# Attention values with the values as weights: outputs as columns, sums by ones, inverses by 32x32 turns

## The chip, the core and the metric

The kernel runs on one core of one Trainium2 chip. The metric is the device time of one execution in microseconds. A core has five engines that run side by side and wait for each other through semaphores: TensorE (matmuls, PE in the profile, its weight loads PEld), VectorE (DVE), ScalarE (ACT), GpSimd (POOL) and SyncE (SP, which here only issues DMAs). TensorE writes to PSUM[...].

## What is computed

For 8 batches and 12 heads of 64, over 448 tokens: q and k are normalised by their root mean square, attention is taken, the heads of a token are put side by side (768), and a feed-forward layer follows with w_in (768 x 2048) and w_out (2048 x 768).

```
q_n, k_n = rmsnorm(q, g_q), rmsnorm(k, g_k)
attn = exp(scale * q_n @ k_n.T);  attn = attn / sum(attn)
x = concat_heads(attn @ v)                  # 3584 x 768
h = x @ w_in
out = (h * sigmoid(1.702 * h)) @ w_out      # 3584 x 768
```

## The kernel before

**Units.** Two heads of one batch make a pair; 48 pairs in all, six for each batch. The six pairs of batch 0 are cut into two half units each (224 queries), the other 42 pairs are one unit (448 queries). Keys come in four chunks of 112 tokens.

**One unit.** The tasks have letters, and the letters stand in the lists that follow. L loads rows (lines 876 to 883). S, R and Q square, reduce and invert the norms; N (line 942) scales the rows; T turns them on TensorE (line 963), KQ and K copy the turned rows out. V casts the values (line 949). C is the score (line 995): keys as weights, 64 rows for each head, queries streamed, so scores come with keys on partitions. E is the exponential on ScalarE (line 1011), written as `att`.

P is the product with the values (line 1021). There the exponentials are the weights (a window of 128 queries) and the values are streamed, 65 columns wide: 64 of a head and one column of ones, which gives the sum. Four chunks of keys accumulate into one window, so there are 32 matmuls in a whole unit and 16 in a half unit, 1536 in all. The output `o` has queries on partitions. A unit's P is cut into `w` (two in a whole unit, one in a half) and x (four of four matmuls each), 96 (unit, w) and 384 tasks. O (line 1034) takes the reciprocal of the sums and multiplies, on VectorE, into `obs`. B (line 1051) turns `obs` on TensorE so that channels lie on partitions, into one of the work banks "w". X (line 1058) copies it to `xT`, on VectorE or ScalarE. The bank for `o` is a single one: the next P with x = 0 waits for the last O.

**The rest.** F is the product with w_in (line 1218), H a tanh on ScalarE, G the gate on VectorE (line 1237); the product with w_out is made partly in the plain way (Y, line 1251) and otherwise in seven products in place of eight (P1 to P7, lines 1315 to 1322, with sums S1 to S5 and copies X1 to X5 and U); the last two batches share the same scheme for w_in (J, line 1601). D stores rows.

**Order.** Every engine's order is written out in the table ORDER from line 218 on: one list of task names for each engine. `od.add(...)` gives each task its engine, a length that the planner assumes, and what it depends on; `run` then emits the tasks in the order of the lists. So TensorE's order is fixed: value products stand between products of the feed-forward layer. For the score the planner assumes `190 * step + 200` (line 1165), for a value task 130 (line 1174). `fill` (line 841) puts matmuls on zeros where the planner sees TensorE idle at the start.

**The weights.** w_in and w_out come in four DMAs each from GpSimd's queue (WI and WO, lines 1203 to 1206), which also cast them. In GpSimd's list WI 0 and 1 stand ahead of all N, WI 2 and 3 between N and V of the first pairs.

Of the kernel before, what the change touches and what calls it, by code (L numbers as in the profile page):

```python
# [8 lines left out]
FP32 = mybir.dt.float32  # L9
# [24 lines left out]
class _Order:  # L34
# [179 lines left out]
    def open(self, name, now):  # L214
# [5 lines left out]
        ('R', 1, 0), ('R', 0, 1), ('R', 0, 0), ('R', 1, 1), 'g', ('N', 0, 1), 'gG', ('N', 0, 0),  # L220
        ('R', 3, 0), ('KQ', 0), ('K', 0), ('R', 2, 0), ('N', 3, 0), ('KQ', 1), ('K', 1), ('KQ',
        3), ('K', 3), ('R', 4, 0), ('V', 0), ('V', 1), ('KQ', 2), ('K', 2), ('O', 0, 0, 0),
        ('V', 2), ('R', 5, 0), ('X', 0, 0), ('O', 1, 0, 0), ('KQ', 4), ('K', 4), ('O', 2, 0, 0),
        ('N', 5, 1), ('X', 1, 0), ('O', 3, 0, 0), ('KQ', 5), ('K', 5), ('X', 2, 0), ('O', 4, 0,
        0), ('X', 3, 0), ('X', 4, 0), ('O', 0, 1, 0), ('R', 6, 0), ('O', 5, 0, 0), ('R', 7, 0),
        ('X', 0, 1), ('X', 5, 0), ('R', 8, 0), ('Q0', 8), ('O', 1, 1, 0), ('G', 0, 1), ('G', 0,
        0), ('O', 2, 1, 0), ('G', 0, 2), ('X', 1, 1), ('G', 0, 3), ('O', 3, 1, 0), ('R', 10, 0),
        ('X', 2, 1), ('O', 4, 1, 0), ('X', 3, 1), ('G', 0, 4), ('X', 4, 1), ('R', 9, 0), ('G',
        0, 5), ('G', 0, 6), ('O', 5, 1, 0), ('KQ', 7), ('K', 7), ('X', 5, 1), ('KQ', 8), ('G',
        0, 7), ('V', 6), ('R', 11, 0), ('G', 0, 8), ('Q0', 11), ('V', 7), ('G', 0, 9), ('G', 0,  # L230
        11), ('O', 6, None, 0), ('N', 11, 1), ('G', 0, 12), ('G', 0, 10), ('KQ', 9), ('O', 7,
        None, 0), ('K', 9), ('R', 12, 0), ('O', 7, None, 1), ('G', 0, 13), ('R', 13, 0), ('O',
        6, None, 1), ('G', 0, 15), ('G', 0, 14), ('X', 6, None), ('R', 14, 0), ('X', 7, None),
        ('V', 9), ('Q0', 14), ('O', 8, None, 0), ('V', 11), ('R', 15, 0), ('O', 9, None, 1),
        ('R', 16, 0), ('O', 8, None, 1), ('N', 12, 0), ('R', 17, 0), ('Q0', 17), ('O', 9, None,
        0), ('V', 10), ('KQ', 12), ('K', 12), ('O', 11, None, 0), ('N', 13, 1), ('X', 9, None),
        ('R', 18, 0), ('O', 11, None, 1), ('KQ', 13), ('K', 13), ('O', 10, None, 0), ('K', 14),
        ('V', 12), ('O', 10, None, 1), ('R', 19, 0), ('R', 20, 0), ('X', 10, None), ('X', 11,
        None), ('Q0', 20), ('O', 12, None, 1), ('O', 12, None, 0), ('G', 1, 0), ('TT', 0, 0),
        ('TT', 1, 0), ('G', 1, 2), ('G', 1, 1), ('G', 1, 3), ('R', 21, 0), ('O', 13, None, 1),  # L240
        ('TT', 0, 1), ('G', 1, 4), ('TT', 1, 1), ('G', 1, 5), ('R', 22, 0), ('K', 15), ('TT', 2,
        0), ('G', 1, 6), ('O', 13, None, 0), ('G', 1, 7), ('G', 1, 8), ('TT', 2, 1), ('X', 12,
        None), ('O', 14, None, 0), ('G', 1, 9), ('G', 1, 10), ('V', 15), ('R', 23, 0), ('Q0',
        23), ('O', 14, None, 1), ('G', 1, 12), ('G', 1, 11), ('O', 15, None, 1), ('V', 16),
        ('G', 1, 13), ('K', 18), ('G', 1, 14), ('O', 15, None, 0), ('V', 17), ('X', 14, None),
        ('G', 1, 15), ('S1', 0, 3), ('S2', 0, 3), ('N', 22, 0), ('K', 19), ('U', 0, 3, 0), ('O',
        16, None, 0), ('S3', 0, 3), ('TT', 3, 0), ('S4', 0, 3), ('O', 16, None, 1), ('R', 24,
        0), ('S1', 0, 5), ('TT', 3, 1), ('O', 17, None, 1), ('R', 25, 0), ('U', 0, 4, 1), ('S2',
        0, 5), ('X1', 0, 5), ('U', 0, 3, 1), ('N', 23, 0), ('K', 20), ('O', 17, None, 0), ('U',
        0, 5, 0), ('R', 26, 0), ('O', 18, None, 1), ('Q0', 26), ('V', 19), ('K', 21), ('O', 18,  # L250
        None, 0), ('X', 17, None), ('S3', 0, 5), ('S4', 0, 5), ('R', 27, 0), ('O', 19, None, 0),
        ('R', 28, 0), ('U', 0, 6, 1), ('G', 2, 0), ('U', 0, 5, 1), ('KQ', 22), ('K', 22), ('N',
        25, 1), ('X', 18, None), ('O', 19, None, 1), ('G', 2, 1), ('R', 29, 0), ('K', 23), ('V',
        21), ('G', 2, 2), ('O', 20, None, 1), ('G', 2, 3), ('Q0', 29), ('G', 2, 4), ('KQ', 24),
        ('O', 20, None, 0), ('G', 2, 5), ('N', 26, 0), ('N', 27, 0), ('O', 21, None, 0), ('G',
        2, 6), ('G', 2, 7), ('R', 30, 0), ('G', 2, 8), ('G', 2, 9), ('O', 21, None, 1), ('X',
        20, None), ('G', 2, 10), ('O', 22, None, 0), ('G', 2, 11), ('R', 32, 0), ('KQ', 25),
        ('G', 2, 12), ('G', 2, 13), ('O', 22, None, 1), ('G', 2, 14), ('G', 2, 15), ('O', 23,
        None, 1), ('S1', 1, 0), ('X', 22, None), ('R', 31, 0), ('O', 23, None, 0), ('S2', 1, 0),
        ('U', 1, 0, 0), ('V', 25), ('KQ', 27), ('Q0', 32), ('S3', 1, 0), ('N', 29, 1), ('O', 24,  # L260
        None, 1), ('N', 30, 1), ('U', 1, 1, 1), ('N', 30, 0), ('S4', 1, 0), ('U', 1, 1, 0),
        ('R', 33, 0), ('O', 24, None, 0), ('X', 23, None), ('U', 1, 0, 1), ('V', 26), ('O', 25,
        None, 0), ('K', 29), ('G', 3, 0), ('R', 34, 0), ('O', 25, None, 1), ('R', 35, 0), ('V',
        27), ('O', 26, None, 1), ('G', 3, 1), ('Q0', 35), ('G', 3, 2), ('O', 26, None, 0), ('G',
        3, 3), ('X', 25, None), ('G', 3, 4), ('G', 3, 5), ('G', 3, 6), ('G', 3, 7), ('KQ', 30),
        ('R', 36, 0), ('K', 30), ('O', 27, None, 1), ('G', 3, 9), ('G', 3, 8), ('G', 3, 10),
        ('KQ', 31), ('O', 27, None, 0), ('K', 31), ('X', 26, None), ('G', 3, 11), ('O', 28,
        None, 1), ('R', 37, 0), ('G', 3, 12), ('G', 3, 13), ('G', 3, 14), ('O', 28, None, 0),
        ('R', 38, 0), ('G', 3, 15), ('O', 29, None, 0), ('S1', 1, 3), ('KQ', 32), ('S2', 1, 3),
        ('Q0', 38), ('K', 32), ('X1', 1, 3), ('U', 1, 3, 0), ('O', 29, None, 1), ('S3', 1, 3),  # L270
        ('S4', 1, 3), ('O', 30, None, 1), ('KQ', 33), ('S5', 1, 2), ('X2', 1, 3), ('N', 36, 1),
        ('N', 35, 1), ('S1', 1, 5), ('S2', 1, 5), ('U', 1, 4, 1), ('O', 30, None, 0), ('R', 39,
        0), ('U', 1, 3, 1), ('O', 31, None, 0), ('K', 35), ('X1', 1, 5), ('KQ', 34), ('K', 34),
        ('U', 1, 5, 0), ('O', 31, None, 1), ('S3', 1, 5), ('X', 30, None), ('X2', 1, 5), ('R',
        40, 0), ('O', 32, None, 1), ('R', 41, 0), ('S4', 1, 5), ('O', 32, None, 0), ('U', 1, 6,
        1), ('Q0', 41), ('U', 1, 6, 0), ('V', 34), ('U', 1, 5, 1), ('G', 4, 0), ('G', 4, 1),
        ('KQ', 36), ('R', 42, 0), ('X', 32, None), ('O', 33, None, 0), ('KQ', 37), ('K', 37),
        ('G', 4, 2), ('O', 33, None, 1), ('G', 4, 3), ('R', 43, 0), ('G', 4, 4), ('V', 35),
        ('K', 38), ('G', 4, 5), ('O', 34, None, 1), ('R', 44, 0), ('Q0', 44), ('G', 4, 6), ('G',
        4, 7), ('KQ', 39), ('O', 34, None, 0), ('G', 4, 9), ('G', 4, 8), ('X', 33, None), ('O',  # L280
        35, None, 1), ('X', 34, None), ('O', 35, None, 0), ('G', 4, 10), ('G', 4, 11), ('N', 42,
        1), ('G', 4, 12), ('O', 36, None, 0), ('G', 4, 13), ('K', 40), ('N', 43, 1), ('G', 4,
        14), ('G', 4, 15), ('S1', 2, 0), ('S2', 2, 0), ('S3', 2, 0), ('X1', 2, 0), ('O', 36,
        None, 1), ('R', 46, 0), ('O', 37, None, 0), ('X2', 2, 0), ('S4', 2, 0), ('X4', 2, 0),
        ('O', 37, None, 1), ('V', 39), ('U', 2, 0, 0), ('X3', 2, 0), ('U', 2, 1, 1), ('U', 2, 0,
        1), ('O', 38, None, 0), ('KQ', 42), ('K', 42), ('KQ', 43), ('R', 45, 0), ('O', 38, None,
        1), ('O', 39, None, 0), ('G', 5, 0), ('G', 5, 1), ('O', 39, None, 1), ('G', 5, 2), ('R',
        47, 0), ('Q0', 47), ('G', 5, 3), ('G', 5, 4), ('O', 40, None, 0), ('X', 39, None), ('N',
        44, 1), ('G', 5, 5), ('O', 40, None, 1), ('G', 5, 6), ('O', 41, None, 0), ('KQ', 44),
        ('N', 46, 0), ('N', 45, 0), ('G', 5, 8), ('G', 5, 7), ('O', 41, None, 1), ('G', 5, 9),  # L290
        ('G', 5, 10), ('O', 42, None, 0), ('G', 5, 11), ('X', 40, None), ('G', 5, 12), ('N', 45,
        1), ('KQ', 46), ('K', 46), ('G', 5, 13), ('O', 42, None, 1), ('X', 41, None), ('O', 43,
# [380 lines left out]
ON = set()  # L673
# [1130 lines left out]
```

## Time and profile before

| what | value |
|---|---|
| median of 3 runs | 445.63 us (443.93 to 445.68) |
| the profiled execution | 445.17 us |
| its span, first to last instruction | 443.4 us |
| mean granted TensorE clock | 0.992 |
| exponentials on ScalarE (L1016) | 147.0 us |
| w_in products on TensorE (L1224) | 122.2 us |
| scaling of rows on GpSimd (L945) | 71.1 us |
| value products on TensorE (L1029) | 68.8 + 12.9 us |
| gates on VectorE (L1247) | 57.7 us |
| reductions on VectorE (L901) | 58.1 us |

The profile is of one execution; the span is the time between its first and last instruction, and 1.8 us lie around it. A group's busy time is the union of its instructions, and a matmul's record includes its way through the array, so matmuls overlap in the records: the distance between the starts of two of them is what one costs in a row. The 40 slices of the page show TensorE at 0.6 to 0.9 of busy time in the first three slices (some 33 us) and at 0.9 or more then, to the last slices. An entry "a <- b" in a group's row is what was written and what was read; the last figure is the idle time ahead of the group's instructions, with what ended it.

In windows of 10 us the core's 16 DMA engines are busy throughout from 10 to 50 us, and GpSimd issues w_in's first two DMAs at 5.53 us, the others at 18.10 and 27.58 us. The first exponential starts at 20.97 us.

### The profile page before, as it was taken

The page shows a single profiled execution, that of the slowest core. Times are in us where ns is not written, and L with a number is a line of the kernel's source. Part 1 is how long each engine was busy: PE and PEld are TensorE (multiplying, and loading weights), DVE is VectorE, ACT ScalarE, POOL GpSimd, SP SyncE. Part 2 cuts the span into 40 slices and gives each one's busy share as a digit, 9 for nine tenths or more (in the row PEclk, how much of TensorE's full clock was granted, in tenths as well). Part 3 has the DMA queues.
Part 4 walks back from the last instruction along what each step waited for, and adds up shares of the span by engine and source line. Part 5 has one row for each costly group of instructions (what it writes and reads, how often), then busy time and mean ns, then how long its engine had stood idle before and what let it go on. Part 6 is the DMA issues. An engine that isn't in the chain of part 4 may idle for free.

```text
span 443.4 us, 10799 instructions
## 1 busy us (share of the span) xinstructions
PE 426.8 (96%) x4286; PEld 262.3 (59%) x4286; DVE 325.2 (73%) x664; ACT 310.6 (70%) x478; POOL 199.5 (45%) x291
## 2 busy tenths in 40 slices
PE   7689999999999999999999999999999989999996
PEld 5457886665565665666555556556556555555563
DVE  3588878688888888777788578786767679756433
ACT  4299997989977788867777848786877635586221
POOL 5389858677653717537654757820632000000000
PEclk9889999999999999999999999999999999999999
DMA  9999949852325416324504354405012003000254
GB/s 216 275 258 236 229 101 200 183 159 79 116 80 164 133 56 207 105 81 123 157 22 143 106 173 115 129 23 158 2 43 79 1 1 108 0 1 2 72 145 123
DMA packets 51091, 51.04 MB, mean 115 GB/s; under 512 B 4320, under 2 KB 51040, under 8 KB 51040
## 3 DMA queue, kind: packets, MB, share of 16 engines
q1 hardware_dynamic: 40912, 41.35, 33.0%
q0 software_dynamic: 7360, 6.29, 8.9%
q10 hardware_dynamic: 2768, 2.70, 1.9%
q8 instruction: 33, 0.54, 0.6%
q14 instruction: 18, 0.15, 0.1%
HBM read 45.61 MB, written 11.01 MB: 128 GB/s over the span
## 4 chain that ended last, share of the span: by engine, by line
PE 89%; DMA 3%; ACT 3%; DVE 2%; issue 1%; POOL 1%; SPq 0%; ACTq 0%; DVEq 0%; POOLq 0%
PE w L1224 24%; PE w L1320 20%; PE o L1029 12%; PE sc L1008 10%; PE b L1320 5%; PE w L968 4%; PE b L1609 4%; PE w L1255 4%; DMA rows<-in_k_dram 3%; PE w L1609 3%; PE w L1055 2%; ACT att L1016 1%; DVE row L945 1%; DVE g L1247 0%; POOL row L945 0%
## 5 line engine op out<-in xcount | busy, mean ns | idle before, releaser
L1016 ACT ACTIVATE att<-sc 112x896 bf16<-112x896 f32 x168 | 147.0, 917 | 31.5 <-PE sc L1008 30.8
L1224 PE MATMUL w<-xt,w_in_s 128*128 128x448 bf16 (+1 forms) x672 | 122.2, 326 | 0.0
L945 POOL TENSOR_TENSOR row<-rows,rs 112x512 bf16<-112x512 f32 x67 | 71.1, 1076 | 41.2 <-PE w L968 29.3
L1029 PEld LDWEIGHTS <-att 112*128 112x128 bf16 x1536 | 68.2, 98 | 27.0 <-issue 10.4
L1224 PEld LDWEIGHTS <-w_in_s 128*128 128x128 bf16 x672 | 60.1, 97 | 40.0 <-issue 7.6
L1247 DVE SCALAR_TENSOR_TENSOR g<-th,w 128x448 bf16<-128x448 f32 x96 | 57.7, 615 | 15.7 <-ACT th L1235 14.7
L1029 PE MATMUL o<-vx,att 112*128 112x65 bf16 x1280 | 68.8, 195 | 0.1
L901 DVE TENSOR_REDUCE ssq<-sq 112x16 f32<-112x1024 f32 (+1 forms) x50 | 58.1, 1167 | 12.9 <-ACT sq L892 12.6
L1235 ACT ACTIVATE th<-w 128x448 f32<-128x448 f32 x96 | 51.6, 546 | 17.9 <-PE w L1224 15.2
L887 POOL TENSOR_TENSOR sq<-rows 112x512 f32<-112x512 f32 x45 | 48.9, 1106 | 7.4 <-ACT qk L980 3.7
L1008 PE MATMUL sc<-qk 64*128 64x448 bf16 (+1 forms) x360 | 47.4, 343 | 0.1
L1040 DVE TENSOR_TENSOR obs<-o,rcp 112x256 bf16<-112x256 f32 x96 | 40.7, 424 | 3.3
L958 POOL TENSOR_TENSOR vx<-rows,ones 112x512 bf16<-112x512 f32 x21 | 23.3, 1109 | 42.8 <-issue 22.8
L968 PE MATMUL w<-ident,row 112*128 112x112 bf16 x384 | 32.7, 216 | 6.8 <-DVE row L945 2.9
L1320 PEld LDWEIGHTS <-late 128*128 128x128 bf16 x304 | 27.6, 97 | 16.9 <-issue 0.7
L1039 DVE RECIPROCAL rcp<-o 112x4 f32<-112x4 f32 x96 | 17.0, 177 | 25.5 <-PE o L1029 24.5
L1320 PEld LDWEIGHTS <-g 128*128 128x128 bf16 x288 | 25.8, 97 | 16.0 <-issue 1.5
L968 PEld LDWEIGHTS <-row 112*128 112x128 bf16 x384 | 23.2, 99 | 15.9 <-issue 5.2
L892 ACT ACTIVATE sq<-rows 112x1024 f32<-112x1024 f32 (+1 forms) x23 | 23.0, 1002 | 11.4 <-DMA rows<-in_q_dram 7.6
L1320 PE MATMUL w<-w_out_s,g 128*128 128x384 bf16 x152 | 29.2, 325 | 0.0
L1320 PE MATMUL w<-late 128*128 128x384 bf16 x144 | 27.7, 325 | 0.0
L934 POOL TENSOR_TENSOR t<-rs 112x48 f32<-112x48 f32 x28 | 7.8, 278 | 41.1 <-DVE rs L922 37.8
(139 smaller groups left out, 604.9 us busy)
## 6 DMA issues: line engine op xcount, KB each, us to landing
rows<-in_q_dram SPq DMA_DIRECT2D x42, 224.0 KB, 3.7
rows<-in_k_dram SPq DMA_DIRECT2D x41, 224.0 KB, 4.3
rows<-in_v_dram SPq DMA_DIRECT2D x41, 224.0 KB, 4.0
w_in_s<-in_moe_w_in_dram POOLq DMA_DIRECT2D x4, 768.0 KB, 15.3
w_out_s<-in_moe_w_out_dram POOLq DMA_DIRECT2D x4, 768.0 KB, 9.5
out_dram<-osb SPq DMA_DIRECT2D x12, 144.0 KB, 2.9
out_dram<-osb SPq DMA_DIRECT2D x10, 168.0 KB, 3.6
out_dram<-osb SPq DMA_DIRECT2D x14, 96.0 KB, 2.6
```

The source lines that it names most:

```text
L887: made = [nc.gpsimd.tensor_tensor(out=sq[i % N_SQ][:SS, g], in0=raw[turn(i, N_RAW, K_RAW)][:SS, g], in1=raw[turn(i, N_RAW, K_RAW)][:SS, g] ...
L901: nc.vector.reduce_sum(out=ssq_of[g0][:SS, i - g0, part], in_=sq[i % N_SQ][:SS, part], axis=AX.X)
L945: return eng.tensor_tensor(out=row_ring[i % N_QKN][:SS, gi].rearrange("p n (h d) -> p h n d", h=2), in0=raw[turn(i, N_RAW, K_RAW)][:SS, gi ...
L968: nc.tensor.transpose(tps[i][:, gi, s, :], row_ring[i % N_QKN][:SS, gi, s, :], ident[:SS, :SS])
L1008: nc.tensor.matmul(sc[:, hp, j * SH:j * SH + n], lhsT=qkw[r, k0:k0 + WIN], rhs=qk[r, 0, qs], start=True, stop=True)
L1016: nc.scalar.activation(out=att[:SS, t, :, :S], in_=sc, func=ACT.Exp)
L1029: nc.tensor.matmul(os_[u, w][:, x, :], lhsT=att_of(u)[:SS, kc, hp, qs * SS:qs * SS + WIN], rhs=vx_ring[turn(i, N_V, K_V)][:SS, hp, kc, :], ...
L1040: nc.vector.tensor_tensor(out=to[:SS, :, w, :] if h is None else to[:SS, :2].rearrange("p n h d -> p (n h) d"), in0=o[:SS, :, :D], in1=rcp ...
L1224: nc.tensor.matmul(gps[b, m][:, j * SH:j * SH + n], lhsT=w_in_s[:, ki, f * 128:(f + 1) * 128], rhs=xT[b][:, ki, lo:lo + n], start=(ki == 0 ...
L1235: nc.scalar.activation(out=th[:, :], in_=gps[b, m][:, :S], func=ACT.Tanh, scale=0.851)
L1247: nc.vector.scalar_tensor_tensor(out=g_of[b // 2][:, f:f + len(g), lo:lo + n], in0=view(ths.pop((b, m))[:, :]), scalar=1.0, in1=view(gps.p ...
L1320: nc.tensor.matmul(held[to], lhsT=lhs[:, ko, :], rhs=y[:, ko, :], start=first and ko == 0, stop=ko == NK - 1, skip_group_check=not first)
```

## The change

The value product is turned round. Values are the weights (64 columns of one head), the exponentials are streamed, 224 queries at a time; so the output has channels on partitions: head 0 on 0 to 63, head 1 on 64 to 127. The two heads write different halves of the same bank. In place of the extra column of ones there is a tile of ones (112 x 64) as a second weight: its product gives the sum of each query, repeated over the 64 partitions of its head. `w` now means a half of the queries, and x tells what is made: 0 and 1 the sums, 2 and 3 the products. A (unit, w) still has 16 matmuls.

OI is new, on VectorE: the sums are turned in blocks of 32x32, so that 32 queries lie on 32 partitions; one column of each block (7 in all) is inverted; and a block that repeats it is turned back. O then multiplies the products with the inverses straight into `xT`. B, X and `obs` are gone; X is left as a name without an engine. `small_p` has one buffer instead of two.

WI waits for N of pairs 1, 3, 2 and 4, and stands behind them in GpSimd's list, with start times of 15.5 to 27 us assumed.

All lists of ORDER are written anew (they take most of the diff). VectorE's has 96 OI more and 35 X less, 16 N instead of 24, 17 V instead of 22, 28 K instead of 31, 26 KQ instead of 28, 41 U instead of 39. ScalarE's has no X (19 before), 35 S instead of 26, 20 K instead of 17, 22 KQ instead of 20. GpSimd's has 80 N instead of 72, 31 V instead of 26, 15 S instead of 24. TensorE's has the same tasks without the 54 B. The first pairs' loads come in another order.

```diff
-    vx_ring = [consts.tile([128, 2, NS, D + 1], BF16, name=f"vx{j}", tag=f"vx{j}")
+    vx_ring = [consts.tile([128, 2, NS, D], BF16, name=f"vx{j}", tag=f"vx{j}")
...
+    ones_b = consts.tile([128, D], BF16)
+    nc.gpsimd.memset(ones_b, 1.0)
...
-    small_p = pool("small", 2)
+    small_p = pool("small", 1)
...
-        hp, qs = (w, x) if h is None else (x % 2, 2 * h + x // 2)
         if x == 0:
-            os_[u, w] = ps_o.tile([128, NS, D + 1], FP32, tag="o", name="o")
-        for kc in range(NS):
-            nc.tensor.matmul(os_[u, w][:, x, :],
-                             lhsT=att_of(u)[:SS, kc, hp, qs * SS:qs * SS + WIN],
-                             rhs=vx_ring[turn(i, N_V, K_V)][:SS, hp, kc, :],
-                             start=(kc == 0), stop=(kc == NS - 1))
+            os_[u, w] = ps_o.tile([128, 2, SH], FP32, tag="o", name="o")
+        lo = (w if h is None else h) * SH
+        for kc in (2 * (x % 2), 2 * (x % 2) + 1):
+            for hp in range(2):
+                to = slice(hp * D, hp * D + D)
+                nc.tensor.matmul(os_[u, w][to, x // 2, :],
+                                 lhsT=ones_b[:SS, :] if x < 2
+                                 else vx_ring[turn(i, N_V, K_V)][:SS, hp, kc, :],
+                                 rhs=att_of(u)[:SS, kc, hp, lo:lo + SH],
+                                 start=(kc == 0), stop=(kc == NS - 1))
+
+    inv = {}
+    NB = SH // 32
+
+    def invert(u, w):
+        o = os_[u, w]
+        spread = small_p.tile([128, SH], FP32, tag="spread", name="spread")
+        rcp = small_p.tile([128, NB], FP32, tag="rcp", name="rcp")
+        back = inv[u, w] = small_p.tile([128, SH], FP32, tag="back", name="back")
+        nc.vector.transpose(out=spread[:, :], in_=o[:, 0, :])
+        nc.vector.reciprocal(out=rcp[:, :],
+                             in_=spread[:, :].rearrange("p (b j) -> p b j", j=32)[:, :, 0])
+        nc.vector.transpose(out=back[:, :].rearrange("p (b j) -> p b j", j=32),
+                            in_=rcp[:, :].to_broadcast([128, NB, 32]))
...
-        nc.vector.reciprocal(out=rcp[:SS, :], in_=o[:SS, :, D])
-        nc.vector.tensor_tensor(
-            out=to[:SS, :, w, :] if h is None else to[:SS, :2].rearrange("p n h d -> p (n h) d"),
-            in0=o[:SS, :, :D], in1=rcp[:SS, :].to_broadcast([SS, NS, D]), op=ALU.mult)
+        to = columns(u) if h is not None else columns(u)[:, w * SH:(w + 1) * SH]
+        return nc.vector.tensor_tensor(out=to, in0=o[:, 1, :], in1=inv.pop((u, w))[:, :], op=ALU.mult)
...
-    def back_pe(u):
...
-    def take_x(u):
...
-                od.add(("P", i, h, w, x), "PE", 130, lambda u=u, w=w, x=x: values(u, w, x),
+                od.add(("P", i, h, w, x), "PE", 191, lambda u=u, w=w, x=x: values(u, w, x),
...
-                       deps=[("E", i, h, t) for t in range(nt)] + [("V", i), ("B", *back_at(u, N_OBS))]
+                       deps=[("E", i, h, t) for t in range(nt)] + [("V", i)]
...
+            od.add(("OI", i, h, w), "DVE", 1000, lambda u=u, w=w: invert(u, w), at - 2,
+                   deps=[("P", i, h, w, 1)])
+            od.add(("O", i, h, w), "DVE", 400, lambda u=u, w=w: divide(u, w), at - 2,
+                   deps=[("P", i, h, w, NS - 1), ("OI", i, h, w)]
+                   + ([("M", b - 3)] if b else []))
+        od.add(("X", i, h), "none", 0, lambda: None, at, deps=[("O", i, h, w) for w in range(nw)])
...
-        od.add(("WI", c), "POOL", 1050, lambda c=c: load_in(c), -50, deps=[("WI", c - 1)], moves=4400.0)
+        od.add(("WI", c), "POOL", 1050, lambda c=c: load_in(c), -50, at=(15500.0, 19000.0, 23000.0, 27000.0)[c],
+               deps=[("WI", c - 1)] + [("N", (1, 3, 2, 4)[c], gi) for gi in range(2)], moves=4400.0)
```

In TensorE's list P now stands in 206 runs of neighbouring tasks (21 of them all four x of a (unit, w), 93 a single task); before it stood in 194. C stands in 102 runs (104 before).

## The prediction

> **What bounds the kernel now.** I read the busy times first, then the chain that ended last (shares, then pieces in order of time), then the groups by form, then the DMA answer for the first 80 us. Busy times and chain:
>
> ```profile
> PE 426.8 (96%) x4286; PEld 262.3 (59%) x4286; DVE 325.2 (73%) x664; ACT 310.6 (70%) x478; POOL 199.5 (45%) x291
> ...
> PE 89%; DMA 3%; ACT 3%; DVE 2%; issue 1%; POOL 1%; SPq 0%; ACTq 0%; DVEq 0%; POOLq 0%
> ```
>
> TensorE sets the end: 89% of the chain. The other 11% (some 49 us) lies mostly at the start; the chain reaches the first w_in matmul of batch 0 at 38.23 us:
>
> ```profile
> 38.02 0.20 PE w L1055 x2
> 38.23 0.77 PE w L1224 x8
> ...
> 40.16 1.53 PE w L1224 x16
> ```
>
> So what the change adds to TensorE is added to the time, unless the start gives something back. The prices on TensorE come from the same chain in mid-kernel (start, length, piece):
>
> ```profile
> 205.60 0.52 PE o L1029 x16
> 206.12 0.48 PE sc L1008 x4
> 206.60 1.24 PE w L1224 x6
> 207.84 0.20 PE w L1055 x4
> 208.04 1.14 PE w L1224 x6
> ```
>
> Three things are to be seen. (1) 16 of today's value matmuls (65 columns) take 0.52 us, 32.5 ns each. (2) A 448-column matmul takes 1.14/6 = 190 ns; the 224-column ones at 40.16 take 1.53/16 = 95.6 ns; a matmul costs its columns. Yet four score matmuls of 448 columns on 64 rows take 0.48 us, not 0.76: two on different halves of the array run abreast, 2 x 0.19 = 0.38, and 0.10 is left over. (3) Six w_in matmuls take 1.24 us right behind a score and 1.14 us behind a back-turn: again 0.10. So entering half-array tiles costs 0.10 us and leaving them 0.10 us.
>
> **TensorE, part by part.** *Value products.* Removed: per (unit, w) 16 matmuls at 32.5 ns = 0.52 us, times 96 = 49.9 us. Added: per (unit, w) again 16, now of 224 columns with 64 output partitions each, in 8 pairs (the two heads, columns 0-63 and 64-127). If a pair runs abreast as the score's pairs do, 8 x 95.6 ns = 0.765 us, times 96 = 73.4 us. Net **+23.5 us**. Half of it is the sums: what was one extra column (65 instead of 64) is now half of all matmuls.
>
> *Back-turns.* B goes: 42 full units at 0.20 us (four turns) and 12 half units at 0.10 us (two) = 9.6 us. Net **-9.6 us**.
>
> *Changes of tile shape.* Today only the scores (64 rows x 128 columns) differ from the rest. In TensorE's written order they stand in 104 runs, with 208 edges. After, the value products are 128 x 64 tiles: they stand in 206 runs, the scores in 102, and walking the new list the shape changes 509 times. That is 301 edges more. The row prices an edge at 0.10 us, but for row tiles only; no instruction of this trace uses column tiles. Bounds: 0 (column tiles of full depth need no drain) and 301 x 0.10 = 30 us. The Trainium skill, "TensorEngine Tiling (Array Packing)", Key Properties, says that a change of tiling mode, not just of tile, drains TensorE. By that rule it is +30 us and the sum of this part is +44 us; by the hope that only row tiles drain, +14 us. The planner's list gives the score 200 ns on top of its streaming, and the new value task (191 = 2 x 95.5) nothing. I take the rule, since the row shows a cost of the same size both in and out whatever stands beside it: **+30 us**.
>
> The same page (Restrictions) says that column tiling switches fast weight load off. Today a 128-column load fits into 32.5 ns; a pair has 95.6 ns for two 64-column loads. "TensorE: Matmul & The Clock Gate", LDWEIGHTS, gives columns/1.2 ns, so an estimate of 53 ns each: hidden if the two halves load side by side, 107 ns per pair in a row, so +11 ns x 768 = +9 us. I take 0 and keep 9 for the range.
>
> Sum on TensorE: 23.5 - 9.6 + 30 = **+44 us**.
>
> **VectorE.** Prices:
>
> ```profile
> L1040 DVE TENSOR_TENSOR obs<-o,rcp 112x256 bf16<-112x256 f32 x96 | 40.7, 424 | 3.3
> L1039 DVE RECIPROCAL rcp<-o 112x4 f32<-112x4 f32 x96 | 17.0, 177 | 25.5 <-PE o L1029 24.5
> ...
> L1618 DVE COPY att<-w 128x448 f32<-128x448 f32 x3 | 1.9, 620 | 1.2 <-PE w L1609 1.1
> ```
>
> From 256 to 448 elements out of PSUM costs 196 ns, about 1 ns an element, so 224 cost some 0.39 us. Removed: 96 x (0.177 + 0.424) = 57.7 us, and 35 X copies (23 x 0.384 + 12 x 0.266 = 12 us). Added per (unit, w): a turn of 224, a reciprocal of 7, a turn back of 224, and a product of 224: 0.39 + 0.18 + 0.39 + 0.39 = 1.35 us, times 96 = 130 us. No row shows a 32x32 turn: at least a copy (0.39), at most twice that (0.78, +75 us in all); I take the copy, which moves as many elements. The new order also takes 8 N (0.84), 5 V (0.68), 3 K and 2 KQ (0.44 and 0.39) off VectorE and puts 2 U on: some -12 us. Total 325 - 70 + 130 - 12 = 373 us, 77% of a 484 us run. It lies beside TensorE.
>
> What waits on it: P of the next (unit, w) needs the only "o" bank, freed by O. The bank was held for 0.52 + 0.60 us and the delays; now for 0.77 (OI begins after half of it) + 0.96 + 0.39. With some 0.6 us of delays and queue that is about 2.7 us x 96 = 260 us, under the span, so other matmuls can cover it outside the start.
>
> **ScalarE and GpSimd.** ScalarE loses 19 X (0.55 = 10 us) and gains 9 squares (1.06), 3 K, 2 KQ: about +2 us, beside TensorE. GpSimd: 8 N and 5 V more, 9 squares (two instructions of 1.1 us each) less: -6 us. Neither bounds.
>
> **The start.** WI 0 and 1 were issued at 5.5 us, before any N; now all four stand behind N on GpSimd's queue, at 15.5 us or later by the list, and each issue (0.89 us) now stands before N and V of the later pairs instead of in an idle stretch. The DMA engines are full there:
>
> ```profile
> q0 software_dynamic: 7133, 6.13, 48.1%
> q1 hardware_dynamic: 9360, 8.95, 43.0%
> ```
>
> In the first 80 us queue 0 held 48.1% = 38.5 us for eight weight transfers, 4.8 us each. Two of them no longer stand among the rows of the first pairs: at most 9.6 us earlier, at least 0 or somewhat below (the total to be loaded is the same, WI 3 and WO come no earlier, and the half units' chain through the single "o" bank is longer). ScalarE's exponentials did not run in earnest before 21 us for want of rows, so I take half: **-5 us**.
>
> **Sum.** Profiled execution 445.17 us (span 443.4 and 1.8 around it; the median shown is 445.63, 0.1% above): 445.2 + 44 - 5 = **484 us**.
>
> **Rivals.**
> *No drain between column and full tiles*: 445.2 + 14 - 5 = 454 us. For it: a value product still uses the same 112 rows as before, only the score halves the rows. Against: the skill's rule, and the 0.10 us on both sides of every score.
> *The pairs do not run abreast*: each pair costs 191 ns, +73 us more: 557 us. For it: two streams over the same 112 partitions, while the score's pairs read different ones. Against: the rows show that the queue starts pairs together.
> *VectorE becomes the bound*: with turns at 0.78 us it would be busy 373 + 75 = 448 us; in the windows its busiest 10 us (40 to 50) are 91% busy, and 448/0.91 = 492; with the "o" waits some 500 us. For it: in-order queue, one bank. Against: it needs twice the row's price.
> *Faster*: one mechanism, the start. No drain, the whole 9.6 us from the earlier rows, and some 9 us of TensorE's waits gone with the hop O, B, X (two handovers and a work bank fewer per unit): 445.2 + 14 - 9.6 - 9 = 441 us. It decides only if the first w_in matmul moves from 38.2 to below about 24 us without a drain; one of the two is not enough.
>
> **Chances.** 484 (474 to 498): 0.56. No drain, 454 (448 to 462): 0.20. Not abreast: 0.08. VectorE: 0.11. Faster: 0.05. This kernel tells 0.5% (2.2 us) from no change. Faster than 443.4: 0.05; within: 0.03 (the low edge of the second case); slower: 0.92. The range for 8 in 10, 449 to 508, takes in the second case and most of VectorE's, and leaves out serial pairs and the faster case.
>
> **What would show it.** In the chain, w_in matmuls right behind value products should take 0.10 us more than behind other work, and 16 value matmuls in a row 0.77 us plus the entry; 0.87 us behind a full tile is the forecast, 1.5 us means serial pairs. TensorE's share of the chain stays near 89%. The turns on VectorE should be near 0.39 us. The first w_in matmul should come at 30 to 36 us. I am wrong if value products cost no edge, if the turns are much longer, or if VectorE's or ScalarE's waits for each other fill the chain.

## The result and the profile after

The changed kernel takes 501.23 us (median of 4 runs, 499.94 to 502.92) against 445.62 us before: the ratio is 1.1283, 95% interval 1.1239 to 1.1327, so it is slower by 12 to 13%. The prediction was 484 us, with 449 to 508 as its range for 8 in 10. The direction and TensorE's part were right; the likeliest value was 17 us too low, and the time lies above the 474 to 498 of the case that was held likeliest.

The page of the kernel after, span, busy times and chain by engine:

```profile
span 499.8 us, 10579 instructions
...
PE 478.2 (96%) x4104; PEld 257.7 (52%) x4104; DVE 377.6 (76%) x802; ACT 316.1 (63%) x474; POOL 189.7 (38%) x281
...
PE 88%; DVE 8%; DMA 2%; issue 1%; ACT 1%; ACTq 0%; DVEq 0%
```

TensorE is still busy for 96% and still carries the chain, with 88%. VectorE's share of the chain has gone from 2% to 8%, some 30 us. That is not 30 us in which TensorE stood: below, the account of TensorE finds some 12 us of waiting for VectorE at value products. The prediction had this part at nothing.

The chain of the kernel after in order of time, in mid-kernel (start, length, piece):

```profile
197.22 0.48 PE sc L1021 x4
197.71 1.24 PE w L1235 x6
198.95 0.51 PE o L1044 x8
199.45 1.24 PE w L1235 x6
...
204.69 0.20 PE w L981 x4
204.89 0.50 PE o L1044 x8
205.39 0.48 PE sc L1021 x4
205.88 0.33 PE o L1044 x4
206.21 0.02 issue
206.23 0.43 DVE spread L1058
206.66 0.02 issue
206.68 0.21 DVE rcp L1059
```

Eight value matmuls of 224 columns take 0.51 us. Eight in a row would be 0.76, four pairs abreast are 0.38, and 0.12 is left for the way in. The six w_in matmuls behind them take 1.24 us, as they did behind a score, in place of 1.14. So the pairs run abreast, and an edge (a change of tile shape) between a column tile and a full tile costs the same 0.10 us as an edge at a score. The last lines show the chain leaving TensorE for the inversion. It stays on VectorE to 212.67 us, yet TensorE goes on with other matmuls in most of that stretch: by the account below it waits 0.5 us in it. The chain names what ended last, and not how long TensorE stood.

VectorE's new work, groups by form (busy, mean ns, idle before):

```profile
L1058 DVE STREAM_TRANSPOSE spread<-o 128x224 f32<-128x224 f32 x96 | 39.8, 415 | 40.9 <-PE o L1044 40.6
L1061 DVE STREAM_TRANSPOSE back<-rcp 128x224 f32<-128x224 f32 x96 | 39.5, 411 | 3.3
L1068 DVE TENSOR_TENSOR xt<-o,back 128x224 bf16<-128x224 f32 x96 | 37.3, 389 | 10.3 <-PE o L1044 6.2
...
L1059 DVE RECIPROCAL rcp<-spread 128x7 f32<-128x7 f32 x96 | 19.3, 201 | 3.3
```

A turn costs 0.41 us, near the 0.39 us estimated for a copy, and not twice that.

**An account of TensorE.** The distance between the starts of two neighbours in TensorE's order can be split into three parts. Work is what is usual between two of that form in a row (189 ns for 448 columns, 162 for 384, 96 for 224, 49 for 112, 33 for 65; 4 ns to the partner of a pair). The edge is up to 94 ns more where the shape changes: a value product starts 283 ns behind a 448-column matmul in place of 189, and another matmul 191 ns behind the last value product in place of 96. The rest is waiting. Filling matmuls on zeros are counted with the waits. The edges counted are the executed ones, a few more than the list has because of the filling matmuls. In us:

| kernel | profiled execution | work | edges (number) | waits and filling |
|---|---|---|---|---|
| before | 445.17 | 384.4 | 19.8 (212) | 33.3 |
| after | 501.57 | 401.7 | 48.7 (521) | 43.9 |
| difference | 56.4 | 17.3 | 28.9 | 10.6 |

Some 7 us before the first matmul's start and behind the last one's are in no column. Of the waits after, 16.9 us lie at value products; before it was 2.2. They are of two kinds. The first pair behind an edge takes 120 ns to the next pair, later pairs 96: 206 runs x 24 ns = 4.9 us belong to the edges rather than to waiting. The other 12 us are true waits for VectorE, and they in turn have two causes. The table of waits (engine, line, waited for: us in total, times, longest) has both; it counts only time in which no record of TensorE runs:

```profile
PE o L1044 <- DVE spread L1058: 6.3, 13, 0.9
PE o L1044 <- DVE xt L1068: 2.7, 10, 0.6
```

The second is the one that the prediction looked at: the sums of the next (unit, w) wait for the single bank, which O frees. The first was not in it: inside one (unit, w) the first product waits until the turn has read the sums out of the same bank. By the distances of starts it is 9.1 us in 24 places, and the wait for the freed bank 2.5 us in 12.

### The profile page after: what moved, and what is told of

Same layout as the page of the kernel before. It is cut to its first block, busy times and chain, and to the rows that moved or that the text cites. A ratio compares the mean times of both kernels' runs of the same rounds, so it can differ in the third digit from the quotient of the medians.

```text
span 499.8 us, 10579 instructions
## 1 busy us (share of the span) xinstructions
PE 478.2 (96%) x4104; PEld 257.7 (52%) x4104; DVE 377.6 (76%) x802; ACT 316.1 (63%) x474; POOL 189.7 (38%) x281
## 4 chain that ended last, share of the span: by engine, by line
PE 88%; DVE 8%; DMA 2%; issue 1%; ACT 1%; ACTq 0%; DVEq 0%
PE w L1235 22%; PE o L1044 19%; PE w L1331 17%; PE sc L1021 8%; PE b L1331 6%; PE w L981 5%; PE b L1620 4%; PE w L1266 3%; DVE spread L1058 2%; PE w L1620 2%; DMA rows<-in_q_dram 1%; DVE back L1061 1%; PE w L872 1%; DVE ssq L914 1%; DVE xt L1068 1%
## 5 line engine op out<-in xcount | busy, mean ns | idle before, releaser
L958 POOL TENSOR_TENSOR row<-rows,rs 112x512 bf16<-112x512 f32 x72 | 76.4, 1075 | 56.4 <-PE w L981 43.5
L1058 DVE STREAM_TRANSPOSE spread<-o 128x224 f32<-128x224 f32 x96 | 39.8, 415 | 40.9 <-PE o L1044 40.6
L1258 DVE SCALAR_TENSOR_TENSOR g<-th,w 128x448 bf16<-128x448 f32 x96 | 57.6, 611 | 11.2 <-ACT th L1246 10.8
L1044 PE MATMUL o<-att,ones_b 112*64 112x224 bf16 x768 | 60.4, 267 | 2.8 <-DVE xt L1068 2.7
L1044 PE MATMUL o<-att,vx 112*64 112x224 bf16 x640 | 52.4, 264 | 6.0 <-DVE spread L1058 5.7
L1044 PEld LDWEIGHTS <-ones_b 112*64 112x64 bf16 x768 | 30.6, 108 | 38.3 <-issue 26.1
L1068 DVE TENSOR_TENSOR xt<-o,back 128x224 bf16<-128x224 f32 x96 | 37.3, 389 | 10.3 <-PE o L1044 6.2
L905 ACT ACTIVATE sq<-rows 112x1024 f32<-112x1024 f32 (+1 forms) x34 | 34.2, 1018 | 15.4 <-DMA rows<-in_k_dram 7.4
L1044 PEld LDWEIGHTS <-vx 112*64 112x64 bf16 x640 | 29.2, 109 | 27.3 <-issue 24.4
L1061 DVE STREAM_TRANSPOSE back<-rcp 128x224 f32<-128x224 f32 x96 | 39.5, 411 | 3.3
L900 POOL TENSOR_TENSOR sq<-rows 112x512 f32<-112x512 f32 x23 | 24.2, 1073 | 16.2 <-DVE xt L1068 10.0
```

The costliest lines, as they stand in the source:

```text
L958: return eng.tensor_tensor(out=row_ring[i % N_QKN][:SS, gi].rearrange("p n (h d) -> p h n d", h=2), in0=raw[turn(i, N_RAW, K_RAW)][:SS, gi ...
L1044: nc.tensor.matmul(os_[u, w][to, x // 2, :], lhsT=ones_b[:SS, :] if x < 2 else vx_ring[turn(i, N_V, K_V)][:SS, hp, kc, :], rhs=att_of(u)[: ...
L1058: nc.vector.transpose(out=spread[:, :], in_=o[:, 0, :])
L1061: nc.vector.transpose(out=back[:, :].rearrange("p (b j) -> p b j", j=32), in_=rcp[:, :].to_broadcast([128, NB, 32]))
L1258: nc.vector.scalar_tensor_tensor(out=g_of[b // 2][:, f:f + len(g), lo:lo + n], in0=view(ths.pop((b, m))[:, :]), scalar=1.0, in1=view(gps.p ...
```

## The experiments

All but two are edits of the changed kernel; the two say so. Three runs leave part of the computation out: full tiles, the inversion left out, and both together. In the cuts of code, angle brackets and dots stand for what is shortened.

**Tile shape: full tiles for the same columns.**

```diff
-            for hp in range(2):
-                to = slice(hp * D, hp * D + D)
-                nc.tensor.matmul(os_[u, w][to, x // 2, :], lhsT=<64 columns of head hp, or ones>,
-                                 rhs=att_of(u)[:SS, kc, hp, lo:lo + SH], ...)
+            nc.tensor.matmul(os_[u, w][:, x // 2, :], lhsT=<128 columns of the values, or ones>,
+                             rhs=att_of(u)[:SS, kc, 0, lo:lo + SH], ...)
```

> Each pair of 64-column value matmuls (and of ones) is one matmul of a 128-column tile over the first head's exponentials, so the second head's own products and sums are left out. Columns streamed by TensorE, VectorE's work, the single o bank and all orders stay; only the tile shape no longer changes at value products. Theory (each change of shape costs 0.094 us): some 309 of 521 edges go, 29 us, so 501 becomes about 472, with matmuls still 95 ns apart. Rival (the time is lost to waits on the inversion and the o bank, and pairs would be cheaper than full tiles): no more than 5 us is gained, 496 or above. Rival (loads of 64 columns were the price): the spacing within a run falls.

Measured: 474.63 us (474.13 to 475.25), 1.0676 of before (1.0635 to 1.0717). The account gives work 399.3, edges 19.8 (212), waits 48.3. The edges fell by 28.9 us, with the slow first pairs by some 34; the waits rose by 4.4, and by 9 without those pairs; the time fell by 27. A part of what the edges cost comes back as waiting for VectorE once TensorE is quicker. This run has half as many matmul instructions and weight loads at the value products too (768 in place of 1536), so it does not part the edges from these by itself; the joined runs below do. Full-tile matmuls took 95 ns each in a row, as a pair of half tiles did: neither the pairs nor the smaller loads were the price inside a run. The chain shows w_out products behind them with no extra 0.10 us (eight w_out matmuls in 1.30 us, behind a score 1.41):

```profile
207.43 0.49 PE sc L1021 x4
207.91 1.41 PE w L1330 x8
209.32 0.39 PE o L1042 x4
209.71 1.30 PE w L1330 x8
```

**The inversion left out.**

```diff
-        nc.vector.transpose(out=spread[:, :], in_=o[:, 0, :])
-        nc.vector.reciprocal(out=rcp[:, :], ...)
-        nc.vector.transpose(out=back[:, :]..., in_=rcp[:, :].to_broadcast([128, NB, 32]))
+        inv[u, w] = flat_one
```

> Both turns and the reciprocal of the sums are left out; the products are multiplied with ones, so nothing is divided. TensorE's work and order stay. Theory (the part of the miss beyond my sum is TensorE waiting for the longer use of the o bank): the 17 us of waits ahead of value products shrink to a few, 485 to 490 in place of 501. Rival (VectorE is the bound, with 99 us of its work gone): 470 or less. Rival (TensorE's work and edges alone): 499 to 501.

Measured: 489.58 us (488.70 to 490.25), ratio 1.1009 (1.0957 to 1.1061). The waits fell from 43.9 to 32.7 us, those at value products from 16.9 to 5.0, which is the slow first pairs alone; work and edges stayed (401.1, 48.6). The chain by engine is TensorE's again:

```profile
PE 92%; DMA 3%; DVE 2%; ACT 1%; issue 1%; SPq 0%; ACTq 0%; DVEq 0%
```

VectorE lost 88 us of busy time (377.6 to 290.0) and the kernel 12 us. So VectorE's throughput is not the bound; what costs is that TensorE waits for the turn of the sums and for the freed bank.

**Both together.** The two edits above in one kernel.

> Both edits at once (second head's products and the division left out). If edges and waits add up: 501 - 29 - 13 = about 459, which is the time before plus the longer streaming (26 us) less the back-turns (9 us). If the waits only come up because the edges delay TensorE, or the other way round: 465 or more, or 450 or less.

Measured: 456.92 us (454.37 to 459.03), ratio 1.0275 (1.0218 to 1.0332); the parts alone were 26.6 and 11.7 us below 501.23, together 44.3. That is 6 us more than the sum of the parts, and outside the spread of the runs: alone, either edit leaves something of the other's cost. Between the profiled executions, 42.5 us apart, the account has some 29 us of edges, some 12 of waits (the slow first pairs among them) and 2 of work; with full tiles alone the waits had risen. What is left above before is 11.6 us, and 13.9 between the profiled executions. It is the longer work, 15 us more (399.3 against 384.4); edges and waits are within 1 us of before.

**Fewer edges, everything computed.** The four value tasks of a (unit, w) moved together in TensorE's list, to the place of the first.

```diff
-        ('P', 6, None, 0, 0), ('C', 7, None, 0), ('F', 0, 10), ('P', 6, None, 0, 1), ('F', 0, 11), ...
+        ('P', 6, None, 0, 0), ('P', 6, None, 0, 1), ('P', 6, None, 0, 2), ('P', 6, None, 0, 3), ...
```

> The changed kernel, complete, with the four tasks of each (unit, w) moved together to the place of the first in TensorE's list; nothing else. Edges in the list 509 -> 338. Theory of edges: 171 x 0.094 = 16 us less, 485, if waits stay as they are. Rival (TensorE then meets the o bank and the exponentials sooner and waits instead): 495 or more.

Measured: 480.78 us (479.66 to 482.83), ratio 1.0819 (1.0770 to 1.0869). Edges 32.7 us (350), 16.0 less; waits 39.2, which is 4.7 less, not more; 110 slow first pairs fewer make 2.6 of it. Sixteen value matmuls now stand in one run:

```profile
197.12 0.89 PE o L1238 x16
198.00 2.38 PE w L1429 x12
```

0.89 us is 0.77 for eight pairs and 0.12 for the way in, where a run of four takes 0.31 to 0.33 in the chain of the kernel after. In the table of waits, TensorE's matmuls have one row left at value products, that for the freed bank:

```profile
PE o L1238 <- DVE xt L1262: 3.5, 13, 0.6
```

The wait for the turn is gone: the products follow the sums at once, and in all 96 (unit, w) the turn comes behind the last product. Waits at other work rose in exchange, so that the waits fall by no more than 4.7 us. The chain by engine:

```profile
PE 77%; DVE 17%; DMA 2%; issue 2%; ACT 1%; ACTq 0%; DVEq 0%
```

VectorE's share of it rose to 17% while the time fell by 20 us, so this share is no measure of what VectorE costs. The kernel is still 8% slower than the one before.

**Joined in twos**, as a second dose.

> The changed kernel, complete, with value tasks joined in twos in TensorE's list (the two of the sums, the two of the products). Edges in the list 509 -> 422, half of what joining all four took away. Edges alone: 87 x 0.094 = 8 us less, 493. If the gain of joining all four came from the o bank being held for less time rather than from edges, the sums and products stay apart here and little is gained: 498 or more.

Measured: 494.22 us (494.04 to 496.26), beside the changed kernel at 500.36 on the same chip. Edges 40.6 us (434), 8.1 less; waits 44.9, 1.0 more. So 87 edges fewer gave 6 us, and 171 fewer gave 20, against 8 and 16 by 0.094 us each: the time follows the edges, and the waits add or take a few us. A part of the unevenness is in the table of waits, where the wait for the turn is as long as after:

```profile
PE o L1238 <- DVE spread L1252: 7.0, 14, 0.6
```

**The inversion behind the last product.** Only the dependency of OI changes; VectorE's list keeps its place.

```diff
-                   deps=[("P", i, h, w, 1)])
+                   deps=[("P", i, h, w, NS - 1)])
```

> The changed kernel, complete, with the inversion's tasks put behind the last product of their (unit, w) instead of behind the sums; all lists stay. In the trace TensorE waited 6.3 us in 13 places for a turn of the sums before it wrote products into the same bank. If those waits count by themselves: 495, and they are gone from the table of waits. Rival (the inversion then starts later and the o bank is held longer): 501 to 506. Where both meet: within 2 us of 501.

Measured: 537.89 us (536.63 to 538.57), ratio 1.2106 (1.2065 to 1.2147): all three expected times missed, by 30 us and more. The waits are 79.6 us, 35.7 more than after. One part came true: TensorE no longer waits for the turn. It waits for the freed bank and for the gates instead, and VectorE for the products:

```profile
DVE spread L1058 <- PE o L1044: 97.0, 73, 5.5
...
PE o L1044 <- DVE xt L1068: 16.8, 38, 1.2
...
PE w L1235 <- DVE g L1258: 8.8, 9, 1.7
```

VectorE waited 40.6 us for value products after, and 97.0 here: OI stands early in its list, and while it waits for the last product the gates and copies behind it stand too. A turn behind the last product is not dear by itself, since with the four tasks joined it stands there in all 96 cases and the kernel is faster. But there sums and products take 0.89 us together, while here other work stands between them. The bank was held for 4.1 us on average, from the first sum to the end of O, against 3.4 after and 3.3 with the tasks joined. A later place for OI in VectorE's list was not tried.

**The start, in the changed kernel.** The four loads of w_in back among the first pairs' work:

```diff
-    ('S', 1, 1), ('N', 0, 1), ('N', 1, 0), ('N', 1, 1), ('N', 2, 0), ('V', 4), ('N', 2, 1), ('WI', 0), ...
+    ('S', 1, 1), ('WI', 0), ('WI', 1), ('N', 0, 1), ('N', 1, 0), ('N', 1, 1), ('WI', 2), ('N', 2, 0), ...
```

> The changed kernel, complete, with the four loads of w_in back where they stood before: two ahead of all N of GpSimd, the others among the N of the first pairs, without their waits. My prediction had the later weights at a gain of 5 us (0 to 9.6): then this takes 506. Rival (the start gained nothing that reaches the end: the first w_in matmul came 3 us sooner, but TensorE had done 3 us less of its own work by 60 us): 499 to 503. Rival (the later weights cost time at the first w_in products): 497 or less.

Measured: 504.17 us, ratio to before 1.1353 (1.1316 to 1.1391), against 1.1283 of the changed kernel from another chip: 3 us, with intervals that touch. Both were therefore run side by side:

> The changed kernel with w_in's loads early, beside the changed kernel on one chip. If the later weights are worth what they are worth in the kernel before (2.7 us of 443.6 there): 2 to 4 us above the run beside it. If nothing: within 1 us of it. If my 5 us: 4.5 or more above it.

> The changed kernel unaltered, on the same chip as the two runs beside it, so that the early weights and the joined pairs are read against it: 499 to 503.

Measured: 504.88 us (503.03 to 505.25) beside 500.36 us (499.95 to 501.21), 4.5 us. The first w_in matmul comes at 37.31 us with the early weights and at 33.80 with the late ones, and the account's waits and filling are 47.7 against 43.0 us. The early weights also got a lower mean granted clock, 0.990 in four of six runs against 0.993 to 0.997. At the same 0.996 it is 503.0 and 503.8 beside 500.4 and 500.6 us: some 3 of the 4.5 us do not go with the clock.

**The start, in the kernel before.** The kernel before with only w_in's loads moved, in two versions; these are the lists of the second:

```diff
-        ('S', 0, 1), ('WI', 0), ('WI', 1), ('N', 1, 0), ('N', 1, 1), ('N', 3, 1), ('WI', 2), ('N', 2, 0), ('N', 2, 1),
-        ('N', 4, 0), ('N', 4, 1), ('WI', 3), ('V', 4), ('V', 3), ('N', 5, 0), ...
+        ('S', 0, 1), ('N', 1, 0), ('N', 1, 1), ('WI', 0), ('N', 3, 1), ('N', 2, 0), ('N', 2, 1), ('WI', 1),
+        ('N', 4, 0), ('N', 4, 1), ('WI', 2), ('V', 4), ('V', 3), ('WI', 3), ('N', 5, 0), ...
```

> The kernel before, complete, with only the four loads of w_in moved later in GpSimd's list (behind N of pairs 2 and 4, V of 3, N of 5). If the rows of the first pairs come up to 9.6 us sooner and TensorE's start moves with them: 436 to 442. If the transfers to be done by 60 us set the start anyway: 444 to 447. If w_in then comes too late for the first products: 448 or more.

> As the run above, but each load one place earlier (behind N of pair 1, 2, 4, V of 3). Same theories; if w_in's arrival is what counts this is 1 to 4 us better than the run above, if the rows' arrival counts it is 1 to 4 us worse, if neither counts the same within 1 us.

Measured: 441.28 us (438.59 to 443.79; ratio 0.9941, 0.9909 to 0.9973) and 440.85 us (439.60 to 442.31; ratio 0.9925, 0.9897 to 0.9953), beside 443.55 us before on that chip. The first is within its expected 436 to 442, and both are a little faster than both kernels; the two agree within 0.5 us, so the exact place counts for little. ScalarE's list before and in the second version shows how it comes: the key rows for which the first exponential waits land sooner, and it starts at 15.23 us in place of 20.97 (start, length, instruction, idle before):

```profile
20.97 0.92 ACT L1018 ACTIVATE att<-sc 112x896 bf16<-112x896 f32 x1 [4.83 <-DMA rows<-in_k_dram]
...
15.23 0.92 ACT L1040 ACTIVATE att<-sc 112x896 bf16<-112x896 f32 x1 [1.37 <-DMA rows<-in_k_dram]
```

The granted clock went with it: 0.74 to 0.84 from 15 to 30 us before, 1.00 in the second version; over the whole run 0.985 to 0.995 before and 0.992 to 1.000 in the two versions. How much of the 2 to 3 us comes by the clock, and how much by the earlier rows directly, was not parted; the two runs of the first version at 0.992 took 442.8 and 443.8 us, no less than before at 0.992.

## Why the prediction came out as it did

- **What bounds** was right: TensorE, 89% of the chain before and 88% after, and what it was given was added to the time. The other 11% before does not lie "mostly at the start": 24 of 49 us lie in the first 40 us.
- **Value products**, +23.5 us: measured +26.6 (48.9 to 75.5 in the account). The pairs run abreast, as the score's rows said. Of the 3 us beyond in the account, 1 is that the old ones took 48.9 and not 49.9, and 2 lie at the ends of runs (full tiles took 73.2). **Back-turns**, -9.6: measured -9.3.
- **Edges**, +30 us by the rule that a change of tiling mode drains TensorE: measured +28.9 in the account, with 4.9 us more for the slow first pairs, which I had not counted; 27 us came back when the shapes were made alike, and 20 when 171 edges were taken out with nothing else changed but TensorE's order. The rule of the Trainium skill ("TensorEngine Tiling (Array Packing)", Key Properties) agrees with this trace for column tiles as well, at 94 ns a change; the rival of 454 us without a drain is out. The loss of fast weight loads (Restrictions, same page), which I kept at 0 to 9 us, did not show in the time inside a run: pairs were 95 ns apart, the pace of full tiles, though a load of 64 columns has a record of 109 ns and one of 128 columns 98. What makes the first pair slow stays open.
- **Start**, -5 us: 4.5 us in the changed kernel, some 3 at the same clock. The first w_in matmul came at 34.9 us, within the 30 to 36 that were forecast. But the 5 us were half of a ceiling of 9.6 us, with no reason for the half, so their being near is partly luck.
- **VectorE**, beside TensorE at no cost: this is the term that was mis-sized. I had it at 373 us of busy time (measured 377.6), the bank's hold at 2.7 us x 96 = 260 us, and wrote that other matmuls could cover it outside the start. The bank was held for 3.4 us x 96 = 330 us, still under the span. Other matmuls did not cover it in the order that was written out: waits and filling rose by 10.6 us though the start gave 4.5, so by some 15; 4.9 of it are the slow first pairs and some 10 are waits for VectorE. Leaving the inversion out took 11.2 us of waits back. The smaller part of the waiting is the one that the prediction named, for the bank to be freed (2.7 us in the table of waits). The larger part (6.3 us) is a second handover that it left out: the products go into the bank from which the turn still reads the sums. The sum over units said that the bank was free often enough; it could not say whether it was free when a value product stood at the head of TensorE's queue.
- The rival "VectorE becomes the bound" named a time, some 500 us, that was met, but not for its reason: the turns cost a copy's 0.41 us and not 0.78, and 88 us less of VectorE's work gave 12 us.
- Of the faster case only the earlier start came true, and at half its size; the drain is there, and TensorE's waits rose where 9 us of them should have gone. Alone, in the kernel before, the later weights are a gain of 0.6 to 0.75%.

The terms as measured are 17.3 (work), 28.9 (edges), 4.9 (first pairs), 10.2 (waits for VectorE and the like) and -4.5 us (start), together 56.8, where 56.4 lie between the two profiled executions. The 10.2 is what is left of the rise in waits when first pairs and start are taken out, so this sum is the account in other words and no second proof of it.

## What to carry to other kernels

Price every change of tile shape in TensorE's written order (here 0.094 us, 309 more of them) before counting the columns saved, and let tiles of one shape stand in long runs; here runs of sixteen won 20 us back and were still not enough. The turned product itself was cheaper than the old one (half of 75.5 us against 48.9); the sums by ones, which had been one column in 65, made it dearer. When a single PSUM bank is handed between two engines, count not only how long it is held in total but what stands in each engine's list while it is held, and count every handover of it: here the one inside a (unit, w) cost more than the one between two. And a transfer that is not needed yet can stand behind those that are: here that part of the change was worth a few us by itself, and was hidden by the rest.

## What was not expected

- The first pair of a run is slower (120 ns to the next, then 96), also where nothing holds it up.
- Two column tiles of one bank start 3 to 4 ns apart, as two row tiles do, though both read the same 112 partitions.
- TensorE waited 6.3 us, in 13 places, for a turn that reads the sums before it wrote products into the other half of the same bank. With the products directly behind the sums it did not wait, and the turn waited for the products. Whether the chip or the program's own dependencies ask for this was not settled.
- Moving one dependency of a VectorE task to a later product, with its place in the list kept, cost 37 us.
